# Soft-capped attention and a gated FFN in one kernel: x split pair by pair, idle matmuls in the first stage, another split of the early work

## The chip, the core and the metric

The kernel runs on one core of one Trainium2 chip. The metric is the device time of one execution in microseconds. Beside TensorE (PE), which does all matrix products, the core has VectorE (DVE), ScalarE (ACT), GpSimd (POOL) and SyncE (SP), whose queue issues nearly all transfers. Each engine works through its own list of instructions in order and waits on semaphores of the others.

## What is computed

The reference, cut to what matters (the inputs are float32 and the weights come as 64-bit floats):

```
batch, heads, seq, dim = 4, 12, 448, 64
scores = q @ k^T / sqrt(64);  scores = cap * tanh(scores / cap)
attn   = exp(scores - max);   attn = attn / (sum(attn) + 1e-9)
x      = (attn @ v), heads side by side          # 1792 x 768
gate   = sigmoid(x @ w_gate);  val = x @ w_val   # 768 -> 1536
out    = (gate * val) @ w_out                    # 1536 -> 768
```

## The kernel before

**Precision.** Products that must be exact to about float32 are made of two parts of each operand, a high part rounded to the fast type fp32r and a low part that holds the rest (`hi` and `lo`, lines 169 to 183). Three fast products (high with low, high with high, low with high) stand for one exact product. `hi` can be asked of GpSimd ("p"), ScalarE ("a") or VectorE; `lo`, a subtraction, of GpSimd or VectorE.

**Attention** goes by pairs of heads, six pairs to a batch, 24 in all. For a pair `n`: `emit_T` (PE transposes q and k into `tp`, ACT makes the high part and DVE the low part of `T`), `emit_S` (four blocks of keys: PE makes scores `sc` in one of two double banks of PSUM, ACT reads them with tanh into `t`), `emit_exp` (ACT, once for each head `j`), `emit_PV` (PE, `pv`), `emit_rd` and `emit_out` (the sums of the softmax are copied to `rd`, inverted on DVE and multiplied into `xraw`). Pairs 0 to 11 ("direct") use plain float32 for `pv`, with a block of ones beside v, so that the sums come out of the same product; pairs 12 to 23 use high and low parts (`emit_P`), with the sums made on POOL. Pairs 0 to 5 run alone on PE ("alone", the first stage); their `pv` lie in the three banks that the FFN uses later (`ps_m`) or in the one bank of `ps_v`. The end of a pair hands `xraw` to `flush_x`, which makes the two parts of x, `xspl`.

**The FFN** goes by batches (`moe(b)`). `h` (18 matmuls for each of 24 units of `w_gate` and `w_val`: six blocks of x times three products), then gate and `gspl` on ACT, DVE and POOL, then `o` (12 units of `w_out`). One tile `xspl` holds x of a batch, so x of batch b+1 is split only when the last `h` of batch b is through. The weight units are loaded as 64-bit words into three buffers (`w64`), made into float32 on ACT and three DVE instructions (`convert_w`, lines 619 to 622), and split (`split_w`) into four buffers (`wspl`), from which they are also written to DRAM (`wd`) for the later batches. Six units (`o.early`) are made during the first stage, with the high part on POOL and the low part on DVE.

**Order.** PE and ACT run in the order in which the code is written: the loop at the end of `_emit` takes turns between the steps of `moe(b)` and of the attention of batch b+1, by the costs that both yield. The other queues are ordered by a scheduler, with `high_priority` moving instructions ahead.

## Time and profile before

| | us |
|---|---|
| runs: median of 3 (lowest, highest) | 779.38 (775.72, 781.02) |
| the profiled execution | 781.58 |
| its span (first to last instruction) | 779.7 |
| PE busy (share of the span) | 752.7 (97%) |
| DVE, ACT, POOL busy | 475.8, 355.2, 197.7 |

The profiled execution lies a little above the runs. "Busy" of PE counts matmuls whose ends are modelled, and a matmul at half the clock is busy for twice as long, so 97% does not mean that 97% of the span is needed. By stages: up to 92 us the first six pairs of heads alone; to 282 us the FFN of batch 0 with the attention of batch 1, and so on; from 596 us the FFN alone. The page's "clock" row counts in tenths of 2.4 GHz; before the first change that the recorder saw, it shows full speed whatever the clock was.

### The profile page before, as it was taken

Reading aid. Unit: us, or ns where it says so; the run is one execution under the profiler, and the core shown is the slowest. Engines: PE = TensorE matmul, PEld = TensorE weight load, DVE = VectorE, ACT = ScalarE, POOL = GpSimd, SP = SyncE. Lnnn points to the kernel's source line nnn. Section 1 sums busy time; section 2 is a strip of 40 time slices with the busy share of each in tenths; the row PEclk is TensorE's granted clock in tenths of the full one; section 3 lists DMA queues with packets and bytes.
Section 4 is the critical chain, followed back from the end, with each engine's and each line's share of the span. In section 5 each row is a group of like instructions: output and inputs, shape, how many; then the busy total and the mean of one; then the engine's idle time right before and its main releaser. Section 6 shows DMA issues by size and latency. Waiting matters only on the chain.

```text
span 779.7 us, 10202 instructions
## 1 busy us (share of the span) xinstructions
PE 752.7 (97%) x3908; PEld 645.3 (83%) x3908; DVE 475.8 (61%) x525; ACT 355.2 (46%) x384; POOL 197.7 (25%) x211
## 2 busy tenths in 40 slices
PE   7999699999999999999999999999987999999997
PEld 5555477877888798988899988888877999999996
DVE  1489648879799976777778737778878011111000
ACT  5799556756665826555644235655540000000000
POOL 1033301111120333535445504443544000000000
PEclk7899799999999999999999999999999999999999
DMA  8578758979989986556567966644477977666451
GB/s 218 124 213 229 222 179 276 323 276 336 322 295 298 329 283 199 185 174 188 180 188 246 276 206 190 200 162 152 147 227 191 344 233 228 218 216 210 157 177 55
DMA packets 133545, 172.99 MB, mean 222 GB/s; under 512 B 86512, under 2 KB 111600, under 8 KB 133488
## 3 DMA queue, kind: packets, MB, share of 16 engines
q1 hardware_dynamic: 132400, 171.83, 69.3%
q8 instruction: 33, 0.54, 0.3%
q10 hardware_dynamic: 1088, 0.43, 0.2%
q14 instruction: 24, 0.20, 0.1%
HBM read 135.27 MB, written 36.18 MB: 220 GB/s over the span
## 4 chain that ended last, share of the span: by engine, by line
PE 91%; DVE 5%; POOL 2%; issue 1%; ACT 1%; POOLq 0%; DVEq 0%
PE h L714 46%; PE o L787 20%; PE pv L366 8%; PE sc L325 8%; PE tp L209 2%; PE pv L376 2%; PE pv L375 2%; ACT t L328 1%; DVE pair L622 1%; PE tp L295 1%; PE warm L74 1%; PE dn L410 1%; PE pv L377 1%; DVE T L182 1%; POOL xspl L174 1%
## 5 line engine op out<-in xcount | busy, mean ns | idle before, releaser
L714 PE MATMUL h<-xspl,wspl 128*128 128x448 f32 x1728 | 379.2, 374 | 0.0
L714 PEld LDWEIGHTS h<-xspl,wspl 128*128 128x128 f32 x1728 | 322.8, 189 | 42.8 <-issue 15.6
L787 PE MATMUL o<-wspl,gspl 128*128 128x384 f32 x864 | 159.4, 338 | 1.5 <-DVE osb L804 1.5
L787 PEld LDWEIGHTS o<-wspl,gspl 128*128 128x128 f32 x864 | 150.5, 188 | 5.9 <-issue 3.5
L328 ACT ACTIVATE t<-sc,scale 112x896 f32<-112x896 f32 (+1 forms) x96 | 91.7, 1005 | 53.2 <-PE sc L325 52.7
L744 ACT ACTIVATE gate<-h 128x448 f32<-128x448 f32 x48 | 26.1, 543 | 170.1 <-PE h L714 165.3
L174 POOL TENSOR_SCALAR gspl<-gate 128x448 fp32r<-128x448 f32 x48 | 34.1, 711 | 255.8 <-DVE gate L747 255.8
L336 ACT ACTIVATE t<-t,capv 112x1792 f32<-112x1792 f32 (+1 forms) x48 | 85.6, 1787 | 0.3
L325 PE MATMUL sc<-T 64*112 64x448 f32 (+1 forms) x576 | 76.0, 394 | 8.9 <-DVE T L182 5.4
L366 PE MATMUL pv<-t,vo 112*128 112x448 f32 x192 | 80.7, 555 | 0.0
L325 PEld LDWEIGHTS sc<-T 64*112 64x112 f32 (+1 forms) x576 | 50.3, 185 | 33.6 <-issue 9.6
L747 DVE SCALAR_TENSOR_TENSOR gate<-gate,h 128x448 f32<-128x448 f32 x48 | 29.6, 616 | 76.1 <-PE h L714 75.8
L418 DVE RECIPROCAL rd<-rd 128x448 f32<-128x448 f32 x24 | 70.7, 2948 | 0.4
L366 PEld LDWEIGHTS pv<-t,vo 112*128 112x128 f32 x192 | 36.3, 194 | 26.7 <-issue 26.1
L182 DVE TENSOR_TENSOR gspl<-gate,gspl 128x448 fp32r<-128x448 f32 x48 | 39.5, 823 | 27.6 <-POOL gspl L174 27.6
L804 DVE TENSOR_SCALAR osb<-o 128x384 f32<-128x384 f32 x22 | 11.9, 557 | 72.5 <-PE o L787 72.5
L348 POOL TENSOR_TENSOR a<-t 128x448 f32<-128x448 f32 x24 | 33.0, 1373 | 80.0 <-ACT t L336 50.2
L182 DVE TENSOR_TENSOR T<-tp,T 128x896 fp32r<-128x896 f32 (+1 forms) x24 | 26.9, 1121 | 37.1 <-ACT T L176 37.0
L182 DVE TENSOR_TENSOR pl<-t,ph 128x1344 fp32r<-128x1344 f32 x24 | 47.6, 1984 | 2.0 <-ACT ph L176 1.9
L176 ACT ACTIVATE ph<-t 128x1792 fp32r<-128x1792 f32 x24 | 40.7, 1696 | 17.6 <-PE pv L377 11.3
L620 DVE TENSOR_SCALAR pair<-pair 128x768 int32<-128x768 int32 x36 | 21.8, 606 | 30.5 <-ACT pair L619 30.3
L622 DVE SCALAR_TENSOR_TENSOR pair<-w,pair 128x768 uint16<-128x768 uint32 x36 | 39.6, 1100 | 0.2
(65 smaller groups left out, 678.8 us busy)
## 6 DMA issues: line engine op xcount, KB each, us to landing
wspl<-wd SPq DMA_DIRECT2D x111, 768.0 KB, 4.4
wd<-wspl SPq DMA_DIRECT2D x36, 768.0 KB, 5.1
w<-in_moe_w_val_dram SPq DMA_DIRECT2D x12, 768.0 KB, 6.5
w<-in_moe_w_gate_dram SPq DMA_DIRECT2D x12, 768.0 KB, 6.1
w<-in_moe_w_out_dram SPq DMA_DIRECT2D x12, 768.0 KB, 6.9
qk<-in_q_dram SPq DMA_DIRECT2D x46, 112.0 KB, 4.5
out_dram<-osb SPq DMA_DIRECT2D x24, 192.0 KB, 3.8
qk<-in_k_dram SPq DMA_DIRECT2D x22, 112.0 KB, 4.0
```

The costliest lines, as they stand in the source:

```text
L174: self.nc.gpsimd.tensor_scalar(dst, src, 1.0, 1.0, ALU.mult, ALU.mult)
L176: self.nc.scalar.activation(dst, src, AF.Copy)
L182: e.tensor_sub(dst, src, hi.bitcast(F32))
L325: nc.tensor.matmul(ps[0:w, j, 0:S], a[rows], r[rows], start=(i == 0), stop=(i == len(ops) - 1))
L328: nc.scalar.activation(Pt[n][0:w, :, m, :], ps[0:w, :, 0:S], AF.Tanh, scale=c["scale"][0:w])
L336: nc.scalar.activation(t, t, AF.Exp, scale=c["cap"][rows])
L348: nc.gpsimd.tensor_add(a, t[:, 0, :], t[:, 1, :])
L366: nc.tensor.matmul(pv, vs[n][0:QC, j * NC + m, :], Pt[n][0:QC, j, m, :], start=(m == 0), stop=(m == NC - 1),)
L418: nc.vector.reciprocal(rd, rd)
L622: nc.vector.scalar_tensor_tensor(half, low.bitcast(U32), 2.0 ** -29, half, ALU.mult, ALU.add)
L714: nc.tensor.matmul(ps, a, r, start=(kk == 0 and i == 0), stop=(kk == KD - 1 and i == 2))
L787: nc.tensor.matmul(ps, a, r, start=(x + kk == 0 and i == 0), stop=(x + kk == KF - 1 and i == 2),)
```

## The change

- In the first load, k and v come in runs of four keys (a row of SBUF holds four neighbouring keys, 1 KB) where they came in single keys (256 bytes); v comes in two transfers; the load of `cap`, which was first in SP's queue, is third.
- `keep_busy(n)` issues n matmuls of the identity into a bank that nobody reads: 4 after the first transposes, 3 + 3 among the scores of pair 0, 8 after the transposes of pair 1.
- `o.early` is 4 (was 6), `KEEP` 4 (was 3): the four early units stay in their buffers and none is read back. The low part of an early unit is POOL's.
- In a pair of the first stage the sums of head 1 are copied by DVE, at high priority, where ACT did it. The product with 1 + EPS (a DVE instruction on `rd` ahead of the reciprocal, in every pair) goes; the last multiplication takes the factor along. Pair 5 has a higher priority, and its second `pv` lies in `ps_v`.
- `xspl` is a ring of six buffers, one for each pair. Blocks 0 to 2 of batch 2 lie in the `w64` buffers, so the first three pairs of batches 2 and 3 can be split at once. The low part of pair 5 is DVE's.
- The first two `h` units run five of their six blocks each and then the sixth, and the attention of batch 1 starts 30 yielded units later.

```diff
-    nc.sync.dma_start(out=capv, in_=cap.partition_broadcast(P))
...
     for src, i in ((k, 1), (q, 0)):
-        _load_inside((nc.sync, nc.scalar), c["qk0"][:, i], src, 0)
+        _load_inside((nc.sync, nc.scalar), c["qk0"][:, i], src, 0, runs=i == 1)
+    nc.sync.dma_start(out=capv, in_=cap.partition_broadcast(P))
     _load_evenly(nc, c["v0"], v, 0)
...
+    def keep_busy(n):
+        for _ in range(n):
+            nc.tensor.matmul(fill, ident, ident, start=True, stop=True)
...
-        if alone(n) and not (j == 1 and n % 2 == 0):
+        if alone(n) and not (j == 1 and n in (0, 2, o.NPAIR - 1)):
             pv = o.ps_m.tile([P, S], F32, tag="m", name=f"pv{n}_{j}")
...
-            nc.scalar.activation(rds[n][half(j)], pvs[n, j][D:2 * D], AF.Copy)
+            if alone(n) and j == 1:
+                with o.tc.high_priority(offset=ahead(n)):
+                    nc.vector.tensor_copy(rds[n][half(j)], pvs[n, j][D:2 * D])
+            else:
+                nc.scalar.activation(rds[n][half(j)], pvs[n, j][D:2 * D], AF.Copy)
...
-            nc.vector.scalar_tensor_tensor(rd, rd, EPS, rd, ALU.mult, ALU.add)
             nc.vector.reciprocal(rd, rd)
...
-        o.lo("v", s[:, 1, :], t, s[:, 0, :])
+        o.lo("p" if u < o.early else "v", s[:, 1, :], t, s[:, 0, :])
...
+    def room(b, p):
+        return moe1_done.get(b - 1) or (b >= 2 and p < W64)
+
     def flush_x():
-        while x_pend and moe1_done.get(x_pend[0][0] - 1):
+        while x_pend and room(*x_pend[0][:2]):
             b, p, xr = x_pend.pop(0)
...
+            pool, tag, bufs = (wp, "w64", W64) if b == 2 and p < W64 else (big, "xspl", KD)
+            xs = pool.tile([P, 2, S], F32R, tag=tag, bufs=bufs, name=f"xspl{b}_{p}")
...
+            last = b == 0 and p == o.NPAIR - 1
+            o.lo("p" if b == 0 and not last else "v", xs[:, 1, :], xr[:, p, :], xs[:, 0, :])
...
+            if b == 0 and f == 0:
+                for which in range(2):
+                    w = next_w(u + which)
+                    ps = ps_m.tile([P, S], F32, tag="m", name=f"h{b}_{which}_{f}")
+                    yield from passes(ps, w, range(KD - 1))
+                    begun.append((ps, w))
```

What this does to the order, at the three places that matter. PE at the start, of the kernel before: transposes `tp` and scores `sc` of pair 0, transposes of pair 1, its scores, and the first `pv`.

```order
L209 MATMUL tp_151<-ident,pair_67 128x112 x8
L325 MATMUL sc_0_164<-T_160 112x448 x6
L325 MATMUL sc_1_172<-T_160 112x448 x6
L325 MATMUL sc_2_180<-T_160 112x448 x6
L325 MATMUL sc_3_188<-T_160 112x448 x6
L209 MATMUL tp_196<-ident,qk_143 128x112 x8
```

The same place of the changed kernel:

```order
L212 MATMUL tp_154<-ident,pair_66 128x112 x8
L263 MATMUL fill<-ident 128x128 x4
L339 MATMUL sc_0_171<-T_163 112x448 x6
L339 MATMUL sc_1_179<-T_163 112x448 x6
L263 MATMUL fill<-ident 128x128 x3
L339 MATMUL sc_2_190<-T_163 112x448 x6
L339 MATMUL sc_3_198<-T_163 112x448 x6
L263 MATMUL fill<-ident 128x128 x3
L212 MATMUL tp_209<-ident,qk_145 128x112 x8
L263 MATMUL fill<-ident 128x128 x8
```

The 18 fills stand in the places where PE waits for ACT or DVE; nothing else moved there. PE at the end of the first stage, before: the last `pv` of pair 5, the scores of pair 6, the transposes of pair 7 and its first scores, and then `h`.

```order
L366 MATMUL pv_1_670<-t_563,vo_559 128x448 x4
L325 MATMUL sc_2_695<-T_610 112x448 x6
L325 MATMUL sc_3_703<-T_610 112x448 x6
L209 MATMUL tp_711<-ident,qk_613 128x112 x8
L325 MATMUL sc_0_734<-T_720 112x448 x6
L325 MATMUL sc_1_742<-T_720 112x448 x6
L714 MATMUL h_0_0_754<-xspl_301,wspl_541 128x448 x18
```

And of the changed kernel (five of the rows of `h` left out):

```order
L380 MATMUL pv_1_684<-t_576,vo_571 128x448 x4
L339 MATMUL sc_2_704<-T_634 112x448 x6
L339 MATMUL sc_3_712<-T_634 112x448 x6
L212 MATMUL tp_720<-ident,qk_637 128x112 x8
L743 MATMUL h_0_0_739<-xspl_0_304,wspl_339 128x448 x3
...
L743 MATMUL h_1_0_766<-xspl_4_654,wspl_428 128x448 x3
L743 MATMUL h_0_0_739<-xspl_5_701,wspl_339 128x448 x3
L743 MATMUL h_1_0_766<-xspl_5_701,wspl_428 128x448 x3
```

Thirty matmuls of `h`, on blocks 0 to 4 of x, now stand where the scores of pair 7 stood, and the block of pair 5 comes after them. DVE at the same place, before: unit w_2 is made into float32, then pair 5's `rd`, a low part of a weight, `T` of pair 7 and at last x of pair 5.

```order
L620 TENSOR_SCALAR pair_67<-pair_67 128x768
L621 SCALAR_TENSOR_TENSOR pair_67<-w_2_461,pair_67 128x768
L622 SCALAR_TENSOR_TENSOR pair_67<-w_2_461,pair_67 128x768
L417 SCALAR_TENSOR_TENSOR rd_686<-rd_686 128x448
L418 RECIPROCAL rd_686<-rd_686 128x448
L182 TENSOR_TENSOR wspl_679<-pair_67,wspl_679 128x768
L182 TENSOR_TENSOR T_720<-tp_711,T_720 128x2x448
L421 TENSOR_TENSOR xraw_296<-pv_0_665,rd_686 64x448
L421 TENSOR_TENSOR xraw_296<-pv_1_670,rd_686 64x448
```

And of the changed kernel:

```order
L647 TENSOR_SCALAR pair_66<-pair_66 128x768
L648 SCALAR_TENSOR_TENSOR pair_66<-w_4_433,pair_66 128x768
L649 SCALAR_TENSOR_TENSOR pair_66<-w_4_433,pair_66 128x768
L407 COPY rd_695<-pv_1_684 64x448
L436 RECIPROCAL rd_695<-rd_695 128x448
L439 SCALAR_TENSOR_TENSOR xraw_300<-pv_0_679,rd_695 64x448
L439 SCALAR_TENSOR_TENSOR xraw_300<-pv_1_684,rd_695 64x448
L185 TENSOR_TENSOR T_729<-tp_720,T_729 128x2x448
L647 TENSOR_SCALAR pair_66<-pair_66 128x768
L185 TENSOR_TENSOR xspl_5_701<-xraw_300,xspl_5_701 128x448
```

x of pair 5 moved ahead of `T` of pair 7, and the low part of a weight is gone from between; two instructions (`T` and the first of the next unit) stand ahead of the low part of x.

## Rows read from the trace of the kernel before

**Rows 1.** Page, part 1: busy us of each engine (share of the span).

```profile
PE 752.7 (97%) x3908; PEld 645.3 (83%) x3908; DVE 475.8 (61%) x525; ACT 355.2 (46%) x384; POOL 197.7 (25%) x211
```

**Rows 2.** Chain that ended last: start us, us, engine, tile, line, instructions merged.

```profile
1.36 4.63 PE warm L74 x20
...
13.93 1.77 PE tp L209 x8
...
17.82 2.21 PE sc L325 x10
20.03 5.35 PE pv L366 x8
28.28 3.02 PE pv L366 x8
31.30 1.41 PE sc L325 x10
...
38.80 3.02 PE pv L366 x8
...
107.17 3.85 PE h L714 x18
```

**Rows 3.** Windows: stretch, length, busy PE, PEld, DVE, ACT, POOL, clock, DMA.

```profile
7.00:11.00 4.00, 2.20 (x15) 1.11 (x13) 1.09 (x1) 1.64 (x2) 0.78 (x2) 0.96 0.97 209
11.00:24.00 13.00, 11.23 (x38) 6.67 (x39) 1.09 (x1) 9.27 (x9) 0.00 (x0) 0.50 0.96 260
81.00:92.00 11.00, 4.78 (x32) 3.20 (x32) 10.03 (x9) 8.08 (x8) 4.88 (x6) 0.72 0.87 254
```

**Rows 4.** Groups by line, ACT: busy us, mean ns of one, idle before.

```profile
L328 ACT ACTIVATE t<-sc,scale 112x896 f32<-112x896 f32 (+1 forms) x96 | 91.7, 1005 | 53.2 <-PE sc L325 52.7
L336 ACT ACTIVATE t<-t,capv 112x1792 f32<-112x1792 f32 (+1 forms) x48 | 85.6, 1787 | 0.3
...
L619 ACT ACTIVATE pair<-w 128x768 f32<-128x768 f32 x36 | 32.7, 908 | 14.3 <-DVE wspl L182 9.7 <-DMA w<-in_moe_w_out_dram 4.7
...
L176 ACT ACTIVATE T<-tp 128x896 fp32r<-128x896 f32 (+1 forms) x24 | 22.7, 947 | 29.2 <-PE tp L209 29.2
...
L391 ACT ACTIVATE rd<-pv 64x448 f32<-64x448 f32 x24 | 13.0, 542 | 7.4 <-PE pv L366 6.9
```

**Rows 5.** Timeline, end of the first stage: start us, us, what, idle before.

```profile
82.83 1.87 DVE L622 SCALAR_TENSOR_TENSOR pair<-w,pair 128x768 uint16<-128x768 uint32 x1
...
85.24 2.95 DVE L418 RECIPROCAL rd<-rd 128x448 f32<-128x448 f32 x1
...
89.92 1.26 DVE L421 TENSOR_TENSOR xraw<-pv,rd 64x448 f32<-64x448 f32 x2
...
90.06 2.21 PE L325 MATMUL sc<-T 64*112 64x448 f32 x10 [4.32 <-DVE T L182]
...
92.19 5.68 PE L714 MATMUL h<-xspl,wspl 128*128 128x448 f32 x18
```

**Rows 6.** Timeline, end of the attention of batch 3.

```profile
572.60 4.26 DVE L182 TENSOR_TENSOR xspl<-xraw,xspl 128x448 fp32r<-128x448 f32 x4
...
581.70 0.44 PE L375 MATMUL pv<-pl,vs 128*128 128x448 f32 x1 [2.70 <-DVE xraw L400]
...
588.74 0.47 PE L375 MATMUL pv<-pl,vs 128*128 128x448 f32 x1 [2.23 <-DVE pl L182]
...
595.76 0.47 PE L410 MATMUL dn<-as,ones 128*128 128x448 f32 x1 [1.74 <-DVE as L182]
```

**Rows 7.** Groups by line: a conversion and T's low part on DVE, POOL's of x.

```profile
L622 DVE SCALAR_TENSOR_TENSOR pair<-w,pair 128x768 uint16<-128x768 uint32 x36 | 39.6, 1100 | 0.2
...
L182 DVE TENSOR_TENSOR T<-tp,T 128x896 fp32r<-128x896 f32 (+1 forms) x24 | 26.9, 1121 | 37.1 <-ACT T L176 37.0
...
L182 POOL TENSOR_TENSOR xspl<-xraw,xspl 128x448 fp32r<-128x448 f32 x6 | 7.4, 1240 | 0.5
```

**Rows 8.** Windows: the FFN of batch 0 without its ends.

```profile
100.00:280.00 180.00, 178.38 (x897) 146.25 (x897) 155.82 (x180) 115.17 (x135) 27.69 (x27) 1.00 0.88 294
```

More of the change, by code (lines that the diff above doesn't have):

```diff
@@ L98, in _pair, with _load_inside, _load_evenly @@
     return src[b, 2 * p:2 * p + 2]
[L101 removed]
+def _load_inside(engines, t, src, n, runs=False):
+    s = _pair(src, n)
+    order = "(p c) d -> p c d" if runs else "(c p) d -> p c d"
+    for h in range(2):
+        engines[h % len(engines)].dma_start(
+            out=t[0:src.shape[2] // NCH, :, h, :], in_=s[h].rearrange(order, c=NCH)
+        )
+def _load_evenly(nc, t, src, n):
     s = _pair(src, n)
     for h in range(2):
[L105 to L115 removed]
+        nc.sync.dma_start(
+            out=t[0:src.shape[2] // NCH, h * NCH:(h + 1) * NCH],
+            in_=s[h].rearrange("(p c) d -> p c d", c=NCH),
+        )
 def _load_v(nc, t, src, n):
@@ L192, in load_qk @@
         if evenly:
-            _load_inside([self.nc.sync], qk[:, 1], self.k, n)
+            _load_inside([self.nc.sync], qk[:, 1], self.k, n, runs=True)
         else:
@@ L246, in alone, with ahead @@
         return n < o.NPAIR
+    def ahead(n):
+        return 3 * AHEAD_OF if n == o.NPAIR - 1 else AHEAD_OF
     o.head = lambda b: 25 if direct(b * o.NPAIR) else 18.5
+    fill = o.ps_m.tile([P, P], F32, tag="m", name="fill")
+    def keep_busy(n):
+        for _ in range(n):
+            nc.tensor.matmul(fill, ident, ident, start=True, stop=True)
     ones_f = ap.tile([P, 3 * D], F32, tag="a", bufs=1, name="ones_f")
@@ L415, in emit_out @@
             nc.scalar.activation(rd, ps, AF.Copy)
-        with o.tc.high_priority(offset=AHEAD_OF):
-            nc.vector.scalar_tensor_tensor(rd, rd, EPS, rd, ALU.mult, ALU.add)
+        share = 1.0 / (1.0 + EPS)
+        with o.tc.high_priority(offset=ahead(n)):
             nc.vector.reciprocal(rd, rd)
```

58 lines of the change are left out of this document (31 added, 27 removed).

## Prediction

> **What bounds the kernel now.** I read the page first: PE is busy for 752.7 of 779.7 us and the other engines for 61% or less [rows 1]. So only two things can give time: stretches in which PE stands still, and stretches in which it works at the lower of its two clocks, 1.2 instead of 2.4 GHz, where the same matmuls count as twice as long a busy time. The windows show where these are. From 100 to 280 us PE is busy for 178.38 of 180 us at full clock [rows 8], and from 282 to 572 and after 596 us it is no different: nothing is to be had there. What is left lies at three places, all of which the change touches.
>
> First, the start. The chain of waits has pv of pair 0 at 5.35 us and later pv at 3.02 for the same eight records [rows 2]; the granted clock from 11 to 24 us is 0.50 [rows 3]. In the 4 us before, PE had 2.20 us of work, in pieces between waits, and then the clock fell [rows 3].
>
> Second, the turn from the first stage to the FFN. Between 81 and 92 us PE is busy for 4.78 of 11 us [rows 3]: the scores of pair 7 wait 4.32 us for DVE's part of T, and h, when it comes, takes 5.68 us at half clock [rows 5] against 3.85 later [rows 2].
>
> Third, the end of the attention of batch 3: three waits of PE for DVE of 2.70, 2.23 and 1.74 us, while DVE first makes four low parts of x in one piece of 4.26 us [rows 6].
>
> Between the first and the second, pairs follow each other every 10.52 us (38.80 less 28.28) [rows 2]. ACT's work on one pair is 4 x 1.005 + 2 x 1.787 + 2 x 0.542 + 0.947 + 0.908 = 10.53 us [rows 4]: ACT sets this pace. PE's own work is 2 x 3.02 + 2 x 1.41 and the transposes, half of 1.77, together 9.75 us [rows 2].
>
> **The change, part by part.**
>
> *Start.* The fills add 18 matmuls. Ten like them, the warm-up, took 4.63 us [rows 2], and its records are as slow as the lower clock makes them, so one costs 0.46 us at 1.2 GHz and about 0.23 at 2.4. The first four fall into the wait for ACT's and DVE's T of pair 0 and bring PE's work between 7 and 11 us from 2.20 [rows 3] to 3.1 us or more; I take it that the clock then stays up. What comes back: the transposes of pair 1 (half of 1.77, 0.9), its scores (2.21 to at most 1.41, 0.8) and its pv (5.35 to 3.02, 2.3) [rows 2], together 4.0 us. The scores of pair 0 mostly wait for tanh and give at most another 0.6. The three fills before the transposes of pair 1 (0.7 us) are half hidden by the wait for a bank, and cost 0.4; the last eight (1.9 us) lie in the wait for T. I take -4.0. Bounds: -4.6, and +1 if the clock falls all the same and fills at 0.46 us stand in the way. `cap` lands later, and the branch hangs on it; the warm-up to 6.0 us covers that. The longer runs of k and v take packets away from queues that the chain doesn't name: nothing.
>
> *Pace.* ACT loses one copy of 0.542 us in each pair [rows 4], so its work is 9.99 us, and PE's 9.75 leaves it the bound by little. I take 10.05 us for 10.52 and four whole periods between the two ends: -1.9. Bounds: 0 (something else holds the pace) and -2.2. DVE takes the copy (no row has it on DVE; between nothing and 0.63, half of the 1.26 for two products of the same size and bank [rows 5]; I take 0.6), and loses the product on rd and the low part of a weight. POOL takes that low part, 768 columns; no row has it. From POOL's 1.24 us for 448 columns [rows 7] it is 2.1 us, at least 1.24. POOL is idle for three quarters of the time, and the first unit is wanted only after the stage.
>
> *Turn.* Of the 11 us PE is idle for 6.2; the slow scores cost 2.21 less 10/12 of 1.41, that is 1.0, and the slow h 5.68 less 3.85, that is 1.8: 9.0 us in all [rows 2, 3, 5]. In the new order PE has after the last pv two blocks of scores (1.4), a short wait and the transposes (together 1.3) and then thirty matmuls of h without pair 5 (30 x 3.85 / 18 = 6.4): 9.1 us of work. In this time x of pair 5 must come: copy 0.6, reciprocal 2.95, two products 1.26, T 1.12, one conversion (at most the 1.87 of the dearest) and a low part of about 0.6, 8.4 us [rows 5, 7], behind whatever is left of the conversion of unit 4. It just fits. The wait ahead of the transposes stays (0.7): -8.3. Bounds: -9.0, and -6 if x of pair 5 is 2.3 us late.
>
> *End of batch 3.* Three of the four low parts (3.2 of 4.26 us [rows 6]) are made earlier, one by one, during h of batch 2, where DVE waits for PE anyway, and a product on rd goes. The waits sum to 6.7 us. All DVE work behind moves up by some 3.8 us, but in the new order a reduction that waits for POOL stands ahead of the instruction that frees the bank, so at the first wait less comes. I take -4.0; bounds -1.6 (the first wait is shortened by that, the others stay) and -6.
>
> *Nothing* for the ring of x, the `w64` places, the later start of batch 1's attention and units 4 and 5 (kept, not read back): they move work inside 100 to 280 us, where PE is full [rows 8]. Their cover is DVE's slack there, 24 us of 180; they add two low parts of a weight to its work there and take six products on rd away.
>
> Sum: -4.0 - 1.9 - 8.3 - 4.0 = -18.2. From the profiled execution, 781.58 us, that is 763.4; it lay 2.2 us above the median, 779.38, so I expect a median of 761.2.
>
> **A rule that speaks against the change.** One conversion on DVE took 1.87 us at 82.83 while POOL made a low part of x [rows 5]; the mean of that instruction is 1.10 us [rows 7]. The change gives POOL more such work. The Trainium skill ("SBUF — State Buffer", Who interferes with whom) says that VectorE and GpSimd share one pair of ports as an exclusive lock: an instruction of VectorE with two SBUF inputs and one of GpSimd that reads SBUF exclude each other for their whole length. By that rule a pair's conversions could stand still for a whole low part. By the row the cost is 0.8 us in a pair. DVE's work on one is at most 2.95 + 1.26 + 1.12 + 0.6 and three conversions of 1.1, together 9.2 us in 10.05, so its slack just takes that up. By the rule it would be up to 2.1 us, 1.3 more than there is. The sum goes by the row; the other case is the second rival.
>
> **The rivals.**
>
> *The clock falls at the start anyway.* For it: from 11 to 24 us PE was busy for 11.23 of 13 us and the clock did not come back [rows 3]. Against it: the fall came after 2.20 of 4 us, which the fills nearly fill. Then the start gives nothing and the fills cost 0.5: 761.2 + 4.5, about 766 us. Chance 0.20. The Trainium skill ("TensorE: Matmul & The Clock Gate", Why this matters for your kernels) asks, against a drop within a kernel, only that PE have no long idle gaps. By that the fills would do nothing; here the clock fell with work of 2.20 us in 4, in pieces, so the trace disagrees.
>
> *DVE falls behind in the first stage.* POOL's low parts stretch the conversions, T of the next pair is late, the pace stays at 10.52, and x of pair 5 is some 1.5 us late at the turn: 761.2 + 1.9 + 1.5, about 765 us. Against it: the slack above, and the reciprocal, DVE's longest piece, shows no stretch in the rows (2.95 us while POOL worked) [rows 5]. Chance 0.15.
>
> *Slower: the weights become the bound of the first FFN.* Units 4 and 5 are now split on ACT and DVE once h runs, into buffers that h itself must free, and everything on DVE queues behind them. DVE is busy for 155.82 of 180 us [rows 8]; if its work there grew by more than 24 us (a seventh), PE would wait a us for each further one, and at 24 + 18 + 8 = 50 us the kernel would be over 1% slower: 790 us. The change adds no such sum. Chance 0.03.
>
> **How the numbers follow.** Forecast 0.60, the rivals 0.20, 0.15 and 0.03, and 0.02 for anything else. The likeliest case alone spans 757 to 764 us. The range from 755 (all the better bounds, and the 1.6 us that PE still stands between 100 and 280 us gone too [rows 8]) to 770 (both of the first rivals, in part) takes in the first three. A difference of 1%, 7.8 us, is about what runs of this kernel can tell from no change; below 771.6 us it is faster. Only both rivals in full with the poor bound at the end of batch 3 come to that line: faster 0.91, within 1% 0.06, slower 0.03.
>
> **What would show it.** Start: clock 1.00 from 11 to 24 us, pv of pair 0 near 3.0 us, the second pv of pair 0 starting near 24 us and not at 28.1. Pace: 10.0 to 10.1 us. Turn: h begins near 78 us, without a wait for T, and its first 18 matmuls at full clock. End of batch 3: waits of PE from 572 us on below 3 us, where they were 6.7. From the turn to there PE's busy time should stay at 99%. The prediction is wrong if the clock is at 0.50 in the first stage, if h waits for x of pair 5 by more than 1 us, or if PE waits for weights in the first FFN.

## The result, and the profile after

| | before | after |
|---|---|---|
| runs: median (lowest, highest) | 778.87 (775.72, 781.02), 4 runs | 766.41 (765.18, 766.99), 4 runs |
| the profiled execution | 781.58 | 766.5 |
| its span | 779.7 | 764.6 |

The ratio of after to before is 0.9841, with a 95% interval from 0.9805 to 0.9878: 12.5 us of the medians, 1.2 to 2.0%. The forecast was 761.2 us, so the direction was right and 5.2 us were missing.

The page of the changed kernel, part 1 (busy us of each engine, share of the span, instructions), answers to [rows 1]:

```profile
PE 746.2 (98%) x3944; PEld 643.9 (84%) x3944; DVE 467.7 (61%) x504; ACT 351.6 (46%) x380; POOL 206.3 (27%) x212
```

The windows of the changed kernel, with the same columns as [rows 3] and [rows 8] (stretch, length, busy PE, PEld, DVE, ACT, POOL, clock, DMA share, GB/s):

```profile
7.00:11.00 4.00, 3.03 (x26) 2.49 (x28) 2.35 (x4) 2.11 (x4) 1.26 (x3) 1.00 0.49 112
11.00:24.00 13.00, 12.51 (x87) 8.55 (x84) 1.09 (x1) 10.95 (x11) 0.00 (x0) 1.00 0.96 274
81.00:92.00 11.00, 10.61 (x53) 9.22 (x54) 10.46 (x13) 4.75 (x7) 1.13 (x2) 1.00 0.68 159
...
100.00:280.00 180.00, 178.77 (x904) 146.32 (x902) 153.64 (x177) 116.72 (x137) 36.33 (x31) 1.00 0.93 303
```

The clock stays at 1.00 where it was 0.50 and 0.72, and between 81 and 92 us PE is busy for 10.61 us where it was busy for 4.78. Between 100 and 280 us PE is as full as before (178.77 us for 178.38).

The timeline of PE in the changed kernel, first stage and turn (start us, us, engine, line, what, and in brackets what it waited for before it), answers to [rows 2] and [rows 5]:

```profile
6.91 0.96 PE L212 MATMUL tp<-ident,pair 112*128 112x112 f32 x8 [1.38 <-DVE scale L84]
...
24.70 3.19 PE L380 MATMUL pv<-t,vo 112*128 112x448 f32 x8
...
34.40 0.99 PE L212 MATMUL tp<-ident,qk 112*128 112x112 f32 x8 [0.49 <-ACT t L342]
35.22 3.19 PE L380 MATMUL pv<-t,vo 112*128 112x448 f32 x8
...
80.35 6.32 PE L743 MATMUL h<-xspl,wspl 128*128 128x448 f32 x30
87.06 4.53 PE L743 MATMUL h<-xspl,wspl 128*128 128x448 f32 x21 [0.39 <-DVE xspl L185]
```

Four things are to be seen here. The first transposes wait 1.38 us for the scale that is made of `cap`. The pairs still follow each other every 10.52 us (35.22 less 24.70), exactly as before. In each of them the transposes wait 0.49 us for a tanh of ACT (`t<-sc`). And `h` begins at 80.35 us where it began at 92.19, and stands still for only 0.39 us, for x of pair 5.

The waits of PE in the changed kernel (us in total, times, longest) and two rows of DVE's timeline answer to [rows 6]:

```profile
PE tp L212 <- ACT t L342: 2.9, 6, 0.5
PE pv L389 <- DVE pl L185: 1.5, 1, 1.5
...
PE pv L389 <- DVE xraw L418: 1.0, 1, 1.0
```

```profile
523.80 1.57 DVE L185 TENSOR_TENSOR xspl<-xraw,xspl 128x448 fp32r<-128x448 f32 x1 [1.05 <-POOL xspl L177]
559.07 1.57 DVE L185 TENSOR_TENSOR xspl<-xraw,xspl 128x448 fp32r<-128x448 f32 x1 [1.48 <-POOL xspl L177]
```

At the end of batch 3's attention 2.5 us of waits for `pl` and `xraw` are left of 6.7, and the low parts of x come one by one, also at 472.75 and 498.55 us, in place of four in a row.

### The profile page after: what moved, and what is told of

It reads as the page before. It is cut to its first block, busy times and chain, and to the rows that moved or that the text cites. A ratio compares the mean times of both kernels' runs of the same rounds, so it can differ in the third digit from the quotient of the medians.

```text
span 764.6 us, 10270 instructions
## 1 busy us (share of the span) xinstructions
PE 746.2 (98%) x3944; PEld 643.9 (84%) x3944; DVE 467.7 (61%) x504; ACT 351.6 (46%) x380; POOL 206.3 (27%) x212
## 4 chain that ended last, share of the span: by engine, by line
PE 81%; DVE 9%; DMA 3%; ACT 2%; issue 2%; POOL 1%; SPq 0%; ACTq 0%; DVEq 0%; POOLq 0%
PE h L743 43%; PE o L827 17%; PE pv L380 7%; PE sc L339 7%; DVE rd L436 2%; DMA w<-in_moe_w_out_dram 2%; PE pv L389 2%; PE pv L390 2%; PE tp L212 2%; DVE pl L185 1%; DMA wd<-wspl 1%; ACT t L342 1%; DVE pair L649 1%; DVE wspl L185 1%; DVE pair L648 1%
## 5 line engine op out<-in xcount | busy, mean ns | idle before, releaser
L177 POOL TENSOR_SCALAR gspl<-gate 128x448 fp32r<-128x448 f32 x48 | 40.8, 850 | 247.3 <-DVE gate L787 247.3
L380 PE MATMUL pv<-t,vo 112*128 112x448 f32 x192 | 78.6, 542 | 0.0
L339 PE MATMUL sc<-T 64*112 64x448 f32 (+1 forms) x576 | 71.9, 380 | 1.0 <-DVE T L185 0.7
L185 DVE TENSOR_TENSOR gspl<-gate,gspl 128x448 fp32r<-128x448 f32 x48 | 36.7, 764 | 23.7 <-POOL gspl L177 23.5
L185 DVE TENSOR_TENSOR pl<-t,ph 128x1344 fp32r<-128x1344 f32 x24 | 45.6, 1899 | 2.4 <-ACT ph L179 1.9
L649 DVE SCALAR_TENSOR_TENSOR pair<-w,pair 128x768 uint16<-128x768 uint32 x36 | 41.7, 1158 | 0.3
L646 ACT ACTIVATE pair<-w 128x768 f32<-128x768 f32 x36 | 32.6, 905 | 16.8 <-DVE wspl L185 8.6
```

Source lines behind the costliest of these rows:

```text
L177: self.nc.gpsimd.tensor_scalar(dst, src, 1.0, 1.0, ALU.mult, ALU.mult)
L185: e.tensor_sub(dst, src, hi.bitcast(F32))
L339: nc.tensor.matmul(ps[0:w, j, 0:S], a[rows], r[rows], start=(i == 0), stop=(i == len(ops) - 1))
L380: nc.tensor.matmul(pv, vs[n][0:QC, j * NC + m, :], Pt[n][0:QC, j, m, :], start=(m == 0), stop=(m == NC - 1),)
L646: nc.scalar.activation(x, top.bitcast(F32), AF.Copy, scale=2.0 ** -112)
L649: nc.vector.scalar_tensor_tensor(half, low.bitcast(U32), 2.0 ** -29, half, ALU.mult, ALU.add)
```

## The experiments

Of all kernels here the median of the runs is given, and from the profile three marks: the start of the second `pv` of pair 0 (in three of them the first of its matmuls), the start of `h`, and the start of the last batch's `o`, from which on every kernel does the same. In the changed kernel they stand at 24.70, 80.35 and 694.48 us. The experiments ran in three sets on three chips, with medians of the kernel before of 778.39, 778.59 and 776.87 us; the changed kernel was not run again beside them. Differences of one or two us to its median of 766.41 are therefore less sure than those of the marks.

### The start: is it the idle matmuls that hold the clock?

First the changed kernel without them:

```diff
     def keep_busy(n):
-        for _ in range(n):
-            nc.tensor.matmul(fill, ident, ident, start=True, stop=True)
+        return
```

> The changed kernel without its 18 idle matmuls; all else, the runs of four keys and the order of the first stage, stays. Theory A (the idle matmuls hold the clock): the granted clock falls to .50 somewhere between 8 and 24 us, the first pv of pair 0 takes 4.5 to 5.4 us instead of 3.27, the second pv of pair 0 starts 2.5 to 4 us later than the 24.70 us of the changed kernel, and the whole takes 769 to 770.5 us. Theory B (the loads in runs of four keys fill PE's gaps by themselves, the idle matmuls do nothing): the clock stays at 1.00, the pv starts within 0.5 us of 24.70, and the whole takes 766 to 767 us, or up to 1 us less, since the last 8 idle matmuls stand 1.96 us long in PE's row.

Measured: 767.86 us (767.63 to 769.63). The windows of this kernel:

```profile
7.00:11.00 4.00, 2.38 (x15) 1.59 (x14) 2.19 (x2) 1.72 (x3) 0.98 (x2) 0.70 0.53 121
11.00:24.00 13.00, 11.31 (x46) 6.13 (x44) 1.09 (x1) 10.10 (x9) 0.00 (x0) 0.70 1.00 277
```

The clock falls to 0.70 on average, the first `pv` of pair 0 takes 4.53 us, the second starts at 26.97, 2.3 us late, and the last `o` at 696.39, 1.9 us late; the medians differ by 1.45 us. Theory A holds in mechanism, with less than it asked for (2.5 to 4 us at the mark, 769 to 770.5 us in all). Then the other side, the kernel before with the idle matmuls alone, and the kernel before once more without any edit:

```diff
     emit_T(0)
+    keep_busy(4)
...
             yield emit_S(n, 0) + emit_S(n, 1)
+        if n == 0:
+            keep_busy(3)
...
             yield emit_S(n, 2) + emit_S(n, 3)
+            if n == 0:
+                keep_busy(3)
             emit_T(n + 1)
+            if n == 0:
+                keep_busy(8)
```

> The kernel before with the 18 idle matmuls of the change in the same four places and nothing else. Two profiles of the kernel before had the second pv of pair 0 at 28.11 and at 26.56 us, with mean clocks of .984 and .982 over the run, and its times spread over 775 to 782 us. Theory A (the idle matmuls alone hold the clock, and the clock of the start is what the spread comes from): granted clock 1.00 from 6 to 24 us, second pv of pair 0 at 24.3 to 25.5 us, 775 to 777.5 us, and a spread of runs of 2 us or less. Theory B (the clock needs the runs of four keys as well): the clock still falls before 24 us, the pv starts at 26 us or later, and the time and its spread are those of the kernel before.

> The kernel before, unchanged, profiled a second time, to tell how much of the 781.58 us of its recorded profile belongs to that one execution. Marks in the recorded profile: second pv of pair 0 starts at 28.28 us, the last batch's output product starts at 711.54 us, its last eviction ends at 774.54 us, and 5.2 us follow up to the span's end at 779.7 us. Theory A (the recorded execution had a stretch that is usually shorter): the time is 777.5 to 779.5 us, and one of the marks up to 711.54 stands 1 to 3 us earlier, at a place that the rows name. Theory B (the marks repeat and only the time after the last eviction varies): each mark within 0.5 us, and the difference lies behind 774.54 us.

Measured: with the idle matmuls 776.32 us (775.41 to 777.96, 10 runs), where the kernel before had 776.87 (775.3 to 780.23, 15 runs) beside it; ratio 0.9989, interval 0.9974 to 1.0004. The second profile of the kernel before has a time of 779.48 us, where the median of its runs was 779.43 (774.83 to 781.32, 10 runs). Its window of the start, and behind it that of the kernel before with idle matmuls:

```profile
11.00:24.00 13.00, 10.98 (x42) 5.99 (x44) 1.09 (x1) 8.98 (x8) 0.00 (x0) 0.69 1.10 271
```

```profile
11.00:24.00 13.00, 12.51 (x84) 8.73 (x85) 1.09 (x1) 10.79 (x11) 0.00 (x0) 1.00 0.90 246
```

The second `pv` of pair 0 starts at 28.11 us in the recorded profile of before (its records at [rows 2] count from 28.28), at 26.56 in the second one, and at 23.36 with the idle matmuls. So the idle matmuls alone hold the clock (theory A of that run, though its runs spread over 2.55 us and not 2); the runs of four keys are not needed for it, and no run shows another gain of theirs: the first `pv` of pair 0 starts at 17.36 us with the idle matmuls and the loads of before, and at 17.48 and 17.86 in the two runs below that have the new loads and `cap` first.

How far the clock falls without idle matmuls is another matter in each execution: at 0.50 through the whole stretch [rows 3] in the one, 0.69 in the other, whose mark is 1.55 us earlier (theory A of the second profile). In 51 executions of the unchanged kernel on the three chips the mean clock ran from 0.980 to 0.995 and the span from 772.9 to 780.1 us; every span of 777.0 us or more came with a clock of 0.986 or less. In all eleven profiles with idle matmuls the clock, once it had come up, stayed at 1.00 to 24 us. What that is worth in the median hangs on how far other executions would have fallen, which is argued here and not shown: it is 3.5 us between the two profiles (last `o` at 705.43 against 708.94), and 0.55 us between the medians of runs made side by side, an interval that holds zero.

The loads of the start were the third part of it:

```diff
     capv = const.tile([P, 1], F32, name="capv")
+    nc.sync.dma_start(out=capv, in_=cap.partition_broadcast(P))
...
-    nc.sync.dma_start(out=capv, in_=cap.partition_broadcast(P))
     _load_evenly(nc, c["v0"], v, 0)
```

> The changed kernel with the load of cap issued first again, ahead of the keys and queries of pair 0, as before the change. In the changed kernel cap's first use on VectorE came at 5.56 us (3.83 before), and the first transposes, which started at 6.91 us, waited 1.38 us for the scale made of it. Theory A (the late cap costs its wait): transposes start at 5.8 to 6.2 us, every later row of the first stage moves by the same 0.7 to 1.1 us, and the whole takes 0.7 to 1.1 us less than the changed kernel. Theory B (keys and queries land that much later behind cap): the transposes wait for the loads instead and start at 6.7 us or later; the whole stays within 0.3 us.

Measured: 765.39 us (763.84 to 766.77). Three rows of the timeline, the first transposes, ACT's first step of a conversion and an `o` of batch 0:

```profile
5.79 1.43 PE L212 MATMUL tp<-ident,pair 112*128 112x112 f32 x8
...
238.88 0.91 ACT L646 ACTIVATE pair<-w 128x768 f32<-128x768 f32 x1 [3.84 <-DMA w<-in_moe_w_out_dram]
...
246.76 1.31 PE L827 MATMUL o<-wspl,gspl 128*128 128x384 f32 x6 [1.07 <-DVE osb L844]
```

The wait for the scale is gone, the transposes start at 5.79 us, and the second `pv` at 23.86, 0.84 us earlier: theory A for the stage. By the last `o` (694.96) the profiled execution had lost it again, 1.07 us of it to a wait for an eviction near 247 us, where DVE was late behind a conversion whose `w_out` unit had landed late (ACT waited 3.84 us for it; in the changed kernel the same step started at 238.06 after 1.82). The medians, 1.0 us apart, don't settle whether this is the rule; a run below, with the same edit in it, has no such wait.

### The pace: what makes a pair last 10.52 us?

```diff
-            if alone(n) and j == 1:
-                with o.tc.high_priority(offset=ahead(n)):
-                    nc.vector.tensor_copy(rds[n][half(j)], pvs[n, j][D:2 * D])
-            else:
-                nc.scalar.activation(rds[n][half(j)], pvs[n, j][D:2 * D], AF.Copy)
+            nc.scalar.activation(rds[n][half(j)], pvs[n, j][D:2 * D], AF.Copy)
```

> The changed kernel with the second denominator copy of each pair of the first batch on ScalarE again, as before the change, in place of VectorE. The recorded forecast: ScalarE's sum sets the pace, so its 0.54 us per pair come back as 10.5 to 11.0 us per pair where 10.05 was expected without it; since the pace was measured at 10.52 us with the copy away, that theory now says 11.06 us per pair, and 2 to 2.7 us more for the whole. Rival (PE's own row of work, with its 0.49 us wait for a bank of the scores, sets the pace, and ScalarE has 0.88 to 1.65 us to spare ahead of one tanh of each pair): 10.52 us per pair, unchanged, the spare time of ScalarE ahead of that tanh shrinks by 0.54 us, and the whole stays within 1 us of the changed kernel.

Measured: 764.3 us (763.72 to 764.82), and in PE's timeline

```profile
24.52 3.19 PE L380 MATMUL pv<-t,vo 112*128 112x448 f32 x8
...
34.22 0.99 PE L212 MATMUL tp<-ident,qk 112*128 112x112 f32 x8 [0.49 <-ACT t L342]
35.04 3.19 PE L380 MATMUL pv<-t,vo 112*128 112x448 f32 x8
```

10.52 us with the copy back on ACT, and the same wait of 0.49. ACT's sum does not set the pace here. The trace of the kernel before, which has both copies on ACT, says the same of it: in the middle of the stage ACT waits 0.16 to 0.19 us in each pair for PE's scores, and PE then 0.31 to 0.33 us for the tanh of them:

```profile
36.75 1.91 ACT L328 ACTIVATE t<-sc,scale 112x896 f32<-112x896 f32 x2 [0.19 <-PE sc L325]
37.82 0.98 PE L209 MATMUL tp<-ident,qk 112*128 112x112 f32 x8 [0.33 <-ACT t L328]
```

The changed kernel is not slower with the copy back on ACT: its median is 2.1 us lower, more than the 1 us that the rival allowed, but its last `o` only 0.44 us earlier (694.04). In this profile the 0.39 us in which `h` waited for x of pair 5 are gone too, since DVE has 0.63 us less in front of it. Next the wait itself; `between` is given for the second head of pairs 1 to 5 and makes the transposes of the next pair, its loads and the exponentials of the first head:

```diff
-            emit_T(n + 1)
...
-            emit_exp(n, 0)
...
                 nc.tensor.matmul(
                     pv, vs[n][0:QC, j * NC + m, :], Pt[n][0:QC, j, m, :], start=(m == 0),
                     stop=(m == NC - 1),
                 )
+                if m == 0 and between:
+                    between()
```

> The changed kernel with the transposes of the next pair, in pairs 1 to 5 of the first batch, put behind the first of the four pv matmuls of the second head instead of ahead of it, and the exponentials of that pair's first head behind the transposes' copy on ScalarE. In the changed kernel the transposes waited 0.49 us in each of six pairs for the bank that a tanh of the scores was still reading. Theory A (the pace is PE's row plus this wait): the wait is gone, the pace falls from 10.52 to 10.0 to 10.1 us per pair, 2.0 to 2.6 us over five pairs, and the whole takes 1.5 to 2.6 us less than the changed kernel (the end of the stage may wait longer for VectorE). Theory B (something else holds the pace, ScalarE or the copies of the transposes): the wait moves to the scores of the next pair, which then wait for the copy of the transposes, and the pace stays at 10.4 to 10.6 us.

Measured: 763.67 us (763.36 to 765.29). PE's timeline:

```profile
23.01 1.02 PE L380 MATMUL pv<-t,vo 112*128 112x448 f32 x2
23.87 0.93 PE L212 MATMUL tp<-ident,qk 112*128 112x112 f32 x8
24.64 2.43 PE L380 MATMUL pv<-t,vo 112*128 112x448 f32 x6
...
33.01 1.02 PE L380 MATMUL pv<-t,vo 112*128 112x448 f32 x2
```

The transposes wait no more, and a pair takes 10.00 us (33.01 less 23.01), over four pairs 10.03. The last `o` starts at 692.20, 2.3 us earlier, and the medians are 2.7 us apart. So the pace was PE's own row of work, 10.03 us, plus 0.49 us for a bank of the scores that the tanh still read. The last two edits in one kernel show what comes next:

> The kernel with the transposes behind the first pv matmul (763.7 us, pace 10.03 us per pair) and with both denominator copies on ScalarE in addition. ScalarE's busy time over two pairs was 18.84 us in 20.07; the copy adds 0.54 us per pair, which makes 9.96 us of 10.03. Theory A (ScalarE is the next bound, and only then is the copy on VectorE worth something): some wait for ScalarE returns on TensorE in the first stage, the pace rises to 10.2 to 10.55 us, and the whole takes 1 to 2.5 us more than 763.7. Theory B (it still fits): the pace stays at 10.0 to 10.1 us, x of pair 5 is ready earlier since VectorE has 0.63 us less before it, and the whole takes 0 to 1.5 us less than 763.7.

Measured: 763.3 us (762.65 to 764.21). The second heads' `pv` start at 23.84, 33.98, 44.46, 54.71 and 65.08 us, 10.31 us apart on average: here the copy does cost 0.28 us in a pair. The window over these four pairs has ACT busy for 39.13 of 41.24 us:

```profile
23.84:65.08 41.24, 41.01 (x194) 21.97 (x192) 31.55 (x25) 39.13 (x40) 16.02 (x17) 1.00 0.69 180
```

Such a share alone doesn't show that ACT holds the pace; the kernel before had a larger one at 10.52 us (40.29 of 42.07). The waits show the way, with those of PE in the rows of its weight loads (PEld):

```profile
39.65 2.95 DVE L434 RECIPROCAL rd<-rd 128x448 f32<-128x448 f32 x1 [1.06 <-ACT rd L407]
44.18 0.79 DVE L654 TENSOR_SCALAR pair<-pair 128x768 int32<-128x768 int32 x1 [0.28 <-ACT pair L653]
...
48.88 0.89 PEld L339 LDWEIGHTS sc<-T 64*112 64x112 f32 x10 [0.27 <-DVE T L185]
```

DVE waits for ACT's copies and then for ACT's step of a conversion, its T comes late by that, and PE's scores wait for T. So theory A for the pace, but by way of DVE. As to the time, the last `o` starts at 693.12 us, 0.92 later than in the run before. 0.83 us of it were lost at the start, where the clock came up later and the first idle matmuls still ran at half of it (1.94 us for what takes 1.07 in the changed kernel), 1.1 in the four pairs; 0.37 came back at the turn, where `h` does not wait for x of pair 5, and the rest behind it.

```profile
8.25 1.94 PE L263 MATMUL fill<-ident 128*128 128x128 f32 x8
```

That the two profiled executions take the same time all the same (763.27 and 763.36 us) is due to the stretch behind the last eviction, 5.4 us for 6.4, so the medians don't tell which kernel is the faster.

### The turn: the products begun without pair 5, and GpSimd's low parts

```diff
-            if b == 0 and f == 0:
+            if False:
                 for which in range(2):
```

> The changed kernel with the first two products of the first expert layer made one after the other again (all six pairs of the first, then the second), where the changed kernel does the first five pairs of both and then the sixth of both; the earlier start of this layer stays. In the changed kernel the first 30 matmul rows ran from 80.35 to 86.67 us and then waited 0.39 us for the low part of x of pair 5, ready at 87.01 us. Theory A (the second product's five pairs cover the wait for that x): PE runs 15 rows up to 83.5 us and then waits 3.2 to 3.6 us for x of pair 5, and the whole takes 2.6 to 3.4 us more. Rival (something behind, weights or the scores of pair 7, is late anyway and absorbs it): the wait appears but the whole takes less than 1.5 us more.

Measured: 769.99 us (768.66 to 770.43). PE's timeline and the window of the turn:

```profile
80.21 3.29 PE L743 MATMUL h<-xspl,wspl 128*128 128x448 f32 x15
...
86.47 9.20 PE L743 MATMUL h<-xspl,wspl 128*128 128x448 f32 x36 [2.97 <-DVE xspl L185]
```

```profile
81.00:92.00 11.00, 8.03 (x33) 6.96 (x31) 8.56 (x9) 3.27 (x5) 0.56 (x1) 0.84 0.55 122
```

The wait of 2.97 us comes as theory A had it, a little under its 3.2 to 3.6. But the last `o` starts 4.63 us later (699.11 for 694.48), and the wait grew by 2.58 only. The clock fell behind it, to 0.84 on average over these 11 us: the 36 rows that follow took 9.20 us, where 21 such rows took 4.53 in the changed kernel, which is 7.8 for 36. So the standstill cost another 1.4 us by the clock. The scores that follow these rows start 4.08 us later than in the changed kernel (95.60 for 91.52); the other 0.55 us were lost behind 110 us and not followed. In the next run PE stands still at the same place for 2.44 us, and the clock does not fall (21 rows in 4.52 us).

```diff
-        o.lo("p" if u < o.early else "v", s[:, 1, :], t, s[:, 0, :])
+        o.lo("v", s[:, 1, :], t, s[:, 0, :])
```

> The changed kernel with the low parts of the four early weight units on VectorE again instead of GpSimd. In the changed kernel GpSimd took 1.82 to 1.84 us for one and VectorE's last step of a conversion took 1.85 to 1.87 us where a two-input GpSimd operation lay beside it, 1.07 us elsewhere; VectorE takes 0.95 us for such a low part. Theory A (the two engines slow each other, so the move to GpSimd gave VectorE little): without it the last conversion steps fall where only GpSimd's x splits lie beside them to 1.07 us, VectorE's busy time from 24 to 92 us rises by less than 2.5 us though 3.8 us of low parts are added, x of pair 5 is ready within 1 us of 87.0 us and the whole stays within 1 us. Theory B (VectorE is relieved by the full 3.8 us): its busy time rises by 3.5 us or more, x of pair 5 comes 1 us later or more, PE waits for it, and the whole takes 1 to 2.5 us more.

Measured: 772.49 us (770.51 to 773.65, 10 runs), ratio to the kernel before 0.9932: 6.1 us, half of the whole gain, hang on this one edit, far more than either theory allowed. The profiled execution was the fastest of the ten (770.51 us), and its last `o` starts 4.78 us late (699.26). DVE's timeline in one pair, the wait of PE behind it, and `h`:

```profile
34.59 1.85 DVE L649 SCALAR_TENSOR_TENSOR pair<-w,pair 128x768 uint16<-128x768 uint32 x1
37.40 0.96 DVE L185 TENSOR_TENSOR wspl<-pair,wspl 128x768 fp32r<-128x768 f32 x1 [0.95 <-POOL wspl L177]
38.27 1.08 DVE L185 TENSOR_TENSOR T<-tp,T 128x896 fp32r<-128x896 f32 x1
...
39.41 1.28 PE L339 MATMUL sc<-T 64*112 64x448 f32 x10 [0.80 <-DVE T L185]
...
92.25 4.52 PE L743 MATMUL h<-xspl,wspl 128*128 128x448 f32 x21 [2.44 <-DVE xspl L185]
```

On DVE a low part stands in a queue: it waits 0.95 us for GpSimd's high part, takes 0.96, and T's low part, which PE is waiting for, stands behind it. PE waits 0.8 to 0.9 us in each of these pairs (39.41, 51.05 and 62.69 us: 11.64 us apart), and 2.44 us for x of pair 5. On GpSimd the same low part takes 1.84 us, and no matmul waits for it. The kernel before had these low parts on DVE as well, but behind the reciprocal, where GpSimd's high part had long been done, and without a wait:

```profile
37.60 0.90 DVE L182 TENSOR_TENSOR wspl<-pair,wspl 128x768 fp32r<-128x768 f32 x1
```

The stretched conversion (1.85 us) is there in the run's kernel too, beside GpSimd's low part of x, so it was not the moved low part that caused it.

### The end of batch 3: the rule or the buffers?

```diff
     def room(b, p):
-        return moe1_done.get(b - 1) or (b >= 2 and p < W64)
+        return moe1_done.get(b - 1)
```

> The changed kernel with the rule for early splitting taken back: the x of batches 2 and 3 waits for the end of the preceding batch's first products again, in buffers of one pair each as in the changed kernel. Theory A (the early splits are what shortened the end of batch 3's attention): the waits for pl and xraw between 550 and 580 us grow from 2.5 us in all back to 5 to 7 us, with a row of several xspl splits in a run on VectorE there, and the whole takes 2.5 to 4.5 us more than the changed kernel's 766.4 us. Rival (the buffer per pair alone did it, or the order of the rows around): the waits stay below 3.5 us and the whole within 1 us.

Measured: 765.59 us (765.26 to 766.24): nothing is lost. DVE's timeline has the splits where the changed kernel has them:

```profile
523.28 1.57 DVE L185 TENSOR_TENSOR xspl<-xraw,xspl 128x448 fp32r<-128x448 f32 x1 [1.06 <-POOL xspl L177]
558.55 1.57 DVE L185 TENSOR_TENSOR xspl<-xraw,xspl 128x448 fp32r<-128x448 f32 x1 [1.48 <-POOL xspl L177]
```

The rule moves the instruction in the code, but DVE's queue is ordered by the scheduler, which left the split where it was, right behind GpSimd's high part. With the one buffer for a batch again (and thus without the places in `w64`, which go with the buffers of a pair):

```diff
-            pool, tag, bufs = (wp, "w64", W64) if b == 2 and p < W64 else (big, "xspl", KD)
-            xs = pool.tile([P, 2, S], F32R, tag=tag, bufs=bufs, name=f"xspl{b}_{p}")
+            if b not in x_spl:
+                x_spl[b] = big.tile([P, 2, KD, S], F32R, tag="xspl", name=f"xspl{b}")
+            xs = x_spl[b][:, :, p, :]
```

> The changed kernel with the split x of a batch in one buffer for all six pairs again, and without the early split (which by itself, taken back alone, cost nothing: 765.6 us against 766.4). Theory A (the buffer per pair is what shortened the end of batch 3's attention: a pair's split may begin when the first products of the batch before have read that pair for the last time): the x of batch 3 is split in a run of four or more again near 560 us, the waits for pl and xraw there grow from 2.5 us in all to 5 to 7 us, and the whole takes 2.5 to 4.5 us more. Theory B (something else shortened it, such as where VectorE stood in its row after the earlier start of the layer): the waits stay below 3.5 us, the whole within 1 us.

Measured: 768.4 us (768.02 to 768.81).

```profile
558.80 4.26 DVE L185 TENSOR_TENSOR xspl<-xraw,xspl 128x448 fp32r<-128x448 f32 x4
...
567.90 0.44 PE L389 MATMUL pv<-pl,vs 128*128 128x448 f32 x1 [2.70 <-DVE xraw L418]
```

The row of four and the wait of 2.70 us are those of before [rows 6], to the hundredth. The waits for `xraw`, `pl` and `as` come to 4.4 us where the changed kernel has 2.5 and before had 6.7, which lies between the two theories; the last `o` starts 2.3 us later, the median is 2.0 us higher. At the place itself more is lost. The same products of this kernel, and behind them those of the changed kernel:

```profile
560.45 3.29 PE L828 MATMUL o<-wspl,gspl 128*128 128x384 f32 x18
...
569.84 4.40 PE L828 MATMUL o<-wspl,gspl 128*128 128x384 f32 x18
```

```profile
561.95 3.29 PE L827 MATMUL o<-wspl,gspl 128*128 128x384 f32 x18
...
569.16 3.31 PE L827 MATMUL o<-wspl,gspl 128*128 128x384 f32 x18
```

This execution came 1.5 us ahead (most of it won between 213 and 250 us, for reasons that this edit doesn't touch) and left 2.3 us behind, so that one buffer cost 3.8 us here, theory A's 2.5 to 4.5: 2.0 by the waits and about 1.5 by the clock, which fell behind the 2.70 us (0.92 on average from 561 to 582 us, and 1.00 in the changed kernel). Behind the same wait in the recorded profile of before it did not fall. What shortened the other two waits of before was not taken apart.

### What the runs spoke for, in one kernel

`cap` first, the transposes behind the first `pv` matmul, and the copy of pair 5 alone on ACT:

```diff
-            if alone(n) and j == 1:
+            if alone(n) and j == 1 and n < o.NPAIR - 1:
```

> The three edits that the runs spoke for, in one kernel: cap's load first, the transposes of the next pair behind the first pv matmul of the second head, and the second denominator copy of pair 5 alone on ScalarE (the last one ahead of the first expert layer, where VectorE is waited for). If they add up: transposes start at 5.8 us (0.8 us gained), the pace is 10.03 us (2.3 us gained), the wait for x of pair 5 shrinks from 0.39 us to 0.1 or none (0.3 us gained), 3.4 us in all: 762.5 to 763.5 us. If the wait of 1.07 us for an eviction that came with cap's load first near 247 us comes here too: 763.5 to 764.5 us.

Measured: 762.03 us (761.48 to 762.19, 5 runs); ratio to before 0.9801, interval 0.9779 to 0.9822, where the changed kernel had 0.9841. That is a little under the 762.5 to 763.5 us expected, beside a kernel before that was also lower in this set. The three add up: `tp` starts at 5.78 us, the second heads' `pv` stand at 22.08, 32.08, 42.15, 52.15 and 62.20 us, and `h` runs its first 51 rows without a wait:

```profile
77.20 10.58 PE L754 MATMUL h<-xspl,wspl 128*128 128x448 f32 x51
```

The last `o` starts at 690.90, 3.6 us before that of the changed kernel. The wait for an eviction near 247 us did not come back.

## Why the prediction was right in direction and 5.2 us off

The marks of the two recorded profiles give a ledger. Up to the end of the last eviction (774.54 and 757.49 us) the changed kernel gained 17.05 us of the 18.2 forecast.

| term | forecast | measured | 
|---|---|---|
| start | -4.0 | -3.4 (28.11 to 24.70) |
| pace | -1.9 | 0 (10.52 and 10.52) |
| turn | -8.3 | about -9.4 (what is left of the 17.05; some 0.4 of it lies between 100 and 280 us) |
| end of batch 3 | -4.0 | -4.2 (6.7 to 2.5 us of waits) |
| behind the last eviction | 0 | +1.95 (5.16 to 7.11) |
| profile to median | -2.2 | -0.1 |

- **Start: right in mechanism, wrong in what it was counted from.** The clock stayed at 1.00, the rival by which it falls anyway did not come, and without the idle matmuls it fell. Two errors of size. "The warm-up to 6.0 us covers that" was wrong: `cap` was first used at 5.56 us where it had been 3.83, and the transposes waited, 0.84 us by the run with `cap` first (0.65 to 0.67 against the five other profiles with the same start, whose mark stands at 24.51 to 24.53). And the larger one: the recorded execution of before was one in which the clock stayed at 0.50 for the whole stretch. Against the second profile, whose time is that kernel's median, the start gave 1.9 us (26.56 to 24.70), not 3.4.
- **"It lay 2.2 us above the median, 779.38, so I expect a median of 761.2."** This step failed. Of the 2.1 us by which the recorded execution exceeded the second one, 1.55 stood in that slow start already. The change takes exactly this away, so the sum held it, and the step took it off a second time. The changed kernel's profile lies 0.1 us from its median.
- **"ACT sets this pace."** This step failed too: the pace did not move when the copy left ACT, nor when it came back. The sum of 10.53 us was made of mean durations over the whole kernel, with a conversion in each pair. The window over four pairs of the kernel before, with ACT's busy time as the fourth after the stretch's length, has 40.29 of 42.07 us, 10.07 a pair, so the agreement with 10.52 was chance:

```profile
28.11:70.18 42.07, 40.80 (x194) 21.91 (x193) 34.69 (x35) 40.29 (x41) 10.58 (x14) 1.00 0.72 197
```

  PE's row was in turn taken too short: 9.75 us for 10.03. And the 0.3 to 0.5 us that the transposes waited in each pair for a tanh were in the trace of before and had no place in the argument. That ACT is close was not wrong: with PE's wait gone, one more copy on it costs 0.28 us in a pair. (That `h` began at 80.35 us and not near 78 is for the most part this pace that did not come.)
- **Turn: right, and for more reasons than were priced.** The order of `h` (2.97 us of waiting without it, and 1.4 by the clock) and the low parts on GpSimd, which the text had priced only as work that finds room there, each carry several us. The latter is worth 4.8 us at the last `o` and 6.1 by the medians in this kernel, since it takes a wait for GpSimd out of DVE's queue ahead of T. The kernel before had these low parts on DVE and the pace of 10.52 us; there they stood elsewhere in the queue. Which of the other edits moved them was not tried; DVE as a whole was not fuller (busy for 57.7 us between 24 and 92 with them, 57.5 in the changed kernel). The rival by which DVE falls behind was thus near, and the edit that it was charged to is what kept it away.
- **A rule that speaks against the change.** Three rows of the changed kernel's timeline:

```profile
70.07 1.07 DVE L649 SCALAR_TENSOR_TENSOR pair<-w,pair 128x768 uint16<-128x768 uint32 x1
...
77.25 1.73 POOL L185 TENSOR_TENSOR xspl<-xraw,xspl 128x448 fp32r<-128x448 f32 x1
...
78.01 1.87 DVE L649 SCALAR_TENSOR_TENSOR pair<-w,pair 128x768 uint16<-128x768 uint32 x1
```

  DVE's last conversion step takes 1.87 us beside a low part of x on GpSimd and 1.07 without, while the reciprocal takes 2.95 us with or without such company. The Trainium skill ("SBUF — State Buffer", Who interferes with whom) has an exclusive lock between an instruction of VectorE with two SBUF inputs and one of GpSimd that reads SBUF. By kind of instruction the trace agrees. In size it is 0.8 us for one conversion and not a whole low part, as the sum had it; the two lay beside each other for 0.97 us only, and GpSimd's part was stretched as well (1.73 us, 1.13 at 65.19 us without a conversion beside it). The low parts of weights, for which the prediction feared it, fell beside the copy and the reciprocal. The four conversion steps that were stretched up to 92 us, and the one of the kernel before [rows 5], lay beside a low part of x.
- **The clock.** The Trainium skill ("TensorE: Matmul & The Clock Gate", Why this matters for your kernels) asks in that section, against a drop within a kernel, only that long gaps of PE be avoided. Here the clock of the start fell in three profiles without idle matmuls, in which PE had work in pieces between waits of 0.4 to 1.2 us, and stayed at 1.00 in those in which the idle matmuls stood in these waits: the trace disagrees with it on the start. At the turn, where one gap of 2.97 us was followed by a fall, it agrees. Between the two the traces differ: behind 2.44 us (low parts on DVE) and behind 2.70 us in the recorded profile of before it stayed, behind 2.70 us in the run with one buffer it fell.
- **End of batch 3: right in size, half wrong in cause.** The rule for early splitting, to which the text owed the earlier low parts, does nothing by itself. The ring of buffers, which the text put at nothing, does 2.0 us of the 4.2 by the waits (and 1.5 more by the clock in the one execution without it); the rest of the 4.2 was not taken apart.
- **Behind the last eviction** 1.95 us were lost that no term held. The work there is the same. In the three profiles of the kernel before and of its variant with idle matmuls this stretch took 5.2 to 5.6 us, in the eleven of the changed kernel and its variants 5.4 to 7.1; the changed kernel's own is the longest of all. The last stores landed 3.2 to 3.6 us after their issue in the changed kernel's profile and 2.5 to 2.9 in the recorded one of before, which is 0.7 of it. Why is open; no run was made for it.

## What to carry to other kernels

A profile is one execution: where the clock of the start differs between executions, take a second profile of the kernel before, and never count an execution's excess over the median beside a term that may contain it. An engine whose summed durations equal the period need not set it: read the window's busy time over whole periods, and look for the one wait that recurs in each period on the engine that is fuller. And when a queue is ordered by a scheduler, ask which buffer an instruction waits for and not where it stands in the code; price a moved instruction by what stands behind it in the queue that it leaves.

## What the hardware showed that was not expected

- The granted clock of one unchanged kernel differs between executions: mean 0.980 to 0.995 in 51 of them on three chips, with spans from 772.9 to 780.1 us; with 18 idle matmuls in 10 runs 0.989 to 0.993 and 773.4 to 776.0 us; with the whole change 0.996 to 0.998 and 763.4 to 765.1 us in 4. In the set that had both, the idle matmuls of the kernel before bought a narrower spread (2.6 us in 10 runs, 4.9 in 15 without) more than a better median (0.55 us, not told from zero).
- One standstill of 2.97 us at the turn, 2.58 us more than in the changed kernel, cost 4.1 us by the end of the rows behind it; the clock was at 0.84 on average over the 11 us around it.
- A GpSimd subtraction of 128 x 448 took 1.13 us, and 1.72 to 1.73 beside VectorE's conversion steps; VectorE's two-input step beside it took 1.85 to 1.87 us for 1.07, its reciprocal 2.95 as ever. GpSimd's subtraction of 128 x 768 took 1.82 to 1.84 us beside a copy and a reciprocal.
